# A cached-attention decode kernel: softmax and value product of the last row block taken group by group

## The chip, the cores and the metric

The kernel runs on 1 core of one Trainium2 chip. The metric is device time in microseconds (us). Before the change it was 705.47 us (median of 4 runs, 705.14 to 706.13).

## The reference, cut to what matters

One decode step of a transformer layer: layer norm, grouped attention against a cache, residual, layer norm, MLP, residual.

```python
q = (layernorm(x) @ wq)                       # 16 query heads of 256, one token
k, v = k_cache, v_cache                       # 8 groups x 32768 rows x 256, bf16, each used by 2 query heads
p = softmax(q @ k.T * 256 ** -0.5)            # over 32768 rows
h = x + (p @ v) @ wo                          # 4096 -> 448
h1 = layernorm(h) @ w1 + b1                   # 448 -> 1792
out = h + (h1 * tanh(softplus(h1))) @ w2      # 1792 -> 448
```

The two caches are 268 MB together and every byte is used once. With the weights the kernel reads 279 MB.

## The kernel before

The 32768 rows are taken in 16 row blocks of 2048 (`NR = 16`). For each row block `r` and group `g`, a 1 MB K tile is loaded, transposed on VectorE (DVE) and multiplied on TensorE (PE); the scores of all 8 groups of a row block gather in one PSUM tile `s`. Then one `chain(r)` makes the softmax of the whole row block: maximum on DVE, combined across partitions on GpSimd (POOL), exponential on ScalarE (ACT). The V products of row block `r - 1` run interleaved with the K work of row block `r`. Each is an `o` tile of 64x512, merged into the running sum `ACC` on DVE.

```python
NKN, NKT, NVN, NO = 4, 3, 4, 3                # ring sizes: K tiles, transposed K, V tiles, o tiles
s_ring = [...]                                # 2 score tiles
for r in range(NR + 1):
    if r == NR: flush_pending()
    for g in range(G):
        if r < NR:  k_unit(g, r)              # load K, transpose, 8 matmuls into s_ring[r % 2]
        if r >= 1:  v_unit(g, r - 1)          # load V, 8 matmuls of 512 columns into o
        ...
    if r < NR: chain(r)                       # softmax of the row block, all groups together
```

In the last pass (`r == NR`) only V products are left. There, each group's product is merged with `ACC`, scaled by the inverse denominator, transposed and projected, in series:

```python
    # v_unit, last row block
    for t2 in range(T // 2):
        nc.tensor.matmul(o[:], lhsT=pt[...64 columns...], rhs=vn[...512 columns...], ...)
    dv(nc.vector.scalar_tensor_tensor(out=ob[:], in0=ACC[:, g, :], scalar=fin["a2"][0:64, 0:1], in1=o[:], ...))
    for dh in range(2):
        nc.tensor.matmul(oT_ps[:, dh, :], lhsT=ob[...], rhs=ident_bf[...2 columns...], ...)   # twice
    nc.scalar.copy(out=og[:], in_=oT_ps[:])
    project(og, [2 * g, 2 * g + 1])           # 4 matmuls of 1x448 into h_ps, with wo
```

After that come the layer norm of `h_ps`, the MLP and the store (called the epilogue below). `ld` issues loads from the SP queue in program order, and `dv` keeps DVE's order as written.

## Time and profile before

| what | before | view |
|---|---|---|
| span of the profiled run | 703.4 us | page, first line |
| DMA stream full, about 427 GB/s | from 66 to about 664 us, ends at 667 | slices, windows |
| last K tile begins its transpose | 645.4 us | timeline |
| first of the last eight V products | 656.4 us | timeline |
| last project matmul ends | 685.4 us | timeline |
| epilogue | 18.0 us | timeline |

The slice rows of the page of before divide the span into 40 slices of 17.6 us; a digit is the busy share in tenths, and PEclk is the granted clock of TensorE.

```profile
PE   2842787777877777787777877787777777777785
...
PEclk9975999999999999999999999999999999999996
DMA  8999999999999999999999999999999999999800
GB/s 328 417 361 330 424 429 424 427 429 425 427 428 426 428 427 425 427 425 428 427 426 428 427 427 427 427 426 427 426 428 425 428 428 425 428 426 426 369 0 1
```

The DMA row is 9 nearly to the end, while PE has slack: the stream is the limit until the second slice from the end. Of the time after its end, 703.4 - 667 = 36 us, none is hidden. The timeline of before shows how the tail is spent (columns: start, duration in us, engine, source line, operation, output and inputs; in brackets the idle time before it and what ended that).

```profile
645.41 2.31 DVE L216 STREAM_TRANSPOSE kt<-kn 128x2048 f32<-128x2048 f32 x1 [2.04 <-DMA kn<-in_A_k_cache_dram]
...
647.77 1.90 PE L224 MATMUL s<-kt,QTall 128*128 128x512 bf16 x8 [1.23 <-DVE kt L216]
...
653.09 0.69 ACT L245 ACTIVATE p<-s,NMrun 128x512 bf16<-128x512 f32 x1 [38.28 <-POOL NMrun L243]
...
656.42 4.68 PE L291 MATMUL o<-kn,pt 128*64 128x512 bf16 x13 [1.46 <-DVE pt L267]
...
684.48 0.92 PE L275 MATMUL h_ps<-wo_sb,og 128*1 128x448 bf16 x4 [0.31 <-ACT og L312]
685.44 0.52 ACT L341 COPY h_sb<-h_ps 1x448 f32<-1x448 f32 x1 [1.01 <-PE h_ps L275]
```

The last K tile is transposed at 645.41. The softmax of the whole row block then takes until 656.4, and only then do the eight last V products start, though about half of their data is there (an estimate from the rates in the windows: 427 GB/s to 664 and 249 to 667 leave about 4.0 of 8.4 MB to land). The line with `o<-kn` is a V product too: the first four of the last V tiles are loaded into K buffers in before. The products end at 684.48 + 0.92 = 685.4.

The windows of before give, for a stretch of time, its length, the busy time of PE, of PE's weight loads, of DVE, ACT and POOL, each with its number of instructions, and then the granted clock, the DMA share and GB/s.

```profile
652.00:656.00 4.00, 0.35 (x2) 0.30 (x2) 1.41 (x7) 1.16 (x4) 0.82 (x4) 1.00 1.01 428
656.00:660.00 4.00, 3.58 (x9) 1.51 (x10) 0.52 (x2) 0.00 (x0) 0.00 (x0) 0.59 1.02 430
660.00:664.00 4.00, 4.00 (x21) 1.50 (x19) 1.33 (x2) 0.16 (x1) 0.00 (x0) 0.99 1.01 426
...
694.00:698.00 4.00, 2.81 (x8) 0.97 (x9) 0.93 (x5) 0.06 (x1) 0.00 (x0) 0.50 0.00 0
```

PE was idle for most of 652 to 656. The clock then fell to half at about 656.7 and came back at about 660.1 (windows). In the epilogue it stayed at half although PE was busy 2.81 of 4 us.

### The profile page before, as it was taken

Reading aid. Unit: us, or ns where it says so; the run is one execution under the profiler, and the core shown is the slowest. Engines: PE = TensorE matmul, PEld = TensorE weight load, DVE = VectorE, ACT = ScalarE, POOL = GpSimd, SP = SyncE. Lnnn points to the kernel's source line nnn. Section 1 sums busy time; section 2 is a strip of 40 time slices with the busy share of each in tenths; the row PEclk is TensorE's granted clock in tenths of the full one; section 3 lists DMA queues with packets and bytes.
Section 4 is the critical chain, followed back from the end, with each engine's and each line's share of the span. In section 5 each row is a group of like instructions: output and inputs, shape, how many; then the busy total and the mean of one; then the engine's idle time right before and its main releaser. Section 6 shows DMA issues by size and latency. Waiting matters only on the chain.

```text
span 703.4 us, 5939 instructions
## 1 busy us (share of the span) xinstructions
PE 513.2 (73%) x2322; PEld 214.1 (30%) x2322; DVE 406.7 (58%) x324; ACT 22.0 (3%) x68; POOL 35.5 (5%) x157
## 2 busy tenths in 40 slices
PE   2842787777877777787777877787777777777785
PEld 2310333333333333233333333333333333333223
DVE  2922565656666575666657575666657565665222
ACT  2000000000000000000000000000000000000000
POOL 1010010000101010100101010100101010100100
PEclk9975999999999999999999999999999999999996
DMA  8999999999999999999999999999999999999800
GB/s 328 417 361 330 424 429 424 427 429 425 427 428 426 428 427 425 427 425 428 427 426 428 427 427 427 427 426 427 426 428 425 428 428 425 428 426 426 369 0 1
DMA packets 45648, 279.39 MB, mean 397 GB/s; under 512 B 6066, under 2 KB 11956, under 8 KB 12404
## 3 DMA queue, kind: packets, MB, share of 16 engines
q1 hardware_dynamic: 45620, 279.01, 95.3%
q8 instruction: 18, 0.29, 0.1%
q14 instruction: 10, 0.08, 0.0%
HBM read 278.99 MB, written 0.00 MB: 397 GB/s over the span
## 4 chain that ended last, share of the span: by engine, by line
DMA 76%; DVE 12%; PE 5%; SPq 5%; issue 1%; POOL 0%; ACT 0%; DVEq 0%; POOLq 0%; ACTq 0%
DMA kn<-in_A_k_cache_dram 76%; DVE kt L216 11%; SPq L72 5%; PE o L291 2%; PE h_ps L275 1%; PE o_ps L370 1%; DVE ob L303 1%; PE h1T_ps L350 1%; PE s L224 0%; PE oT_ps L307 0%; ACT p L245 0%; DVE hn_bf L143 0%; DVEq L216 0%; DVE pt L267 0%; DVE g L232 0%
## 5 line engine op out<-in xcount | busy, mean ns | idle before, releaser
L216 DVE STREAM_TRANSPOSE kt<-kn 128x2048 f32<-128x2048 f32 x128 | 295.6, 2310 | 208.8 <-DMA kn<-in_A_k_cache_dram 208.3
L224 PE MATMUL s<-kt,QTall 128*128 128x512 bf16 x1024 | 248.1, 384 | 164.4 <-DVE kt L216 164.4
L291 PE MATMUL o<-vn,pt 128*64 128x512 bf16 x992 | 239.9, 384 | 0.2
L224 PEld LDWEIGHTS <-QTall 128*128 128x128 bf16 x1024 | 98.2, 97 | 311.2 <-issue 192.9
L291 PEld LDWEIGHTS <-pt 128*64 128x64 bf16 x1024 | 102.6, 110 | 139.6 <-issue 52.7
L299 DVE SCALAR_TENSOR_TENSOR ACC<-ACC,alpha_all,o 64x512 f32<-64x512 f32 x112 | 78.2, 698 | 1.7 <-PE o L291 1.7
L234 POOL COPY g<-g 32x1 f32<-32x1 f32 x48 | 8.4, 176 | 609.9 <-DVE g L232 608.3
L245 ACT ACTIVATE p<-s,NMrun 128x512 bf16<-128x512 f32 x16 | 11.0, 688 | 622.4 <-POOL NMrun L243 622.4
L232 DVE TENSOR_REDUCE g<-s 128x1 f32<-128x512 f32 x16 | 11.1, 692 | 23.4 <-PE s L224 23.4
L303 DVE SCALAR_TENSOR_TENSOR ob<-ACC,a,o 64x512 bf16<-64x512 f32 x8 | 5.9, 739 | 21.6 <-PE o L291 21.6
L270 DVE STREAM_TRANSPOSE pt<-p 128x512 bf16<-128x512 bf16 x15 | 10.7, 711 | 9.5 <-ACT p L245 9.5
L291 PE MATMUL o<-kn,pt 128*64 128x512 bf16 x32 | 9.9, 448 | 1.5 <-DVE pt L267 1.5
L243 POOL COPY NMrun<-NMrun 32x1 f32<-32x1 f32 x48 | 8.6, 178 | 2.3
L177 PE MATMUL qT_ps<-xnT,vn 128*128 128x1 bf16 (+1 forms) x128 | 4.0, 165 | 5.4 <-DMA vn<-in_A_wq_dram 5.4
L275 PE MATMUL h_ps<-wo_sb,og 128*1 128x448 bf16 x32 | 7.3, 351 | 0.3 <-ACT og L312 0.3
L370 PE MATMUL o_ps<-w_sb,actT 128*1 128x448 bf16 x14 | 5.4, 574 | 1.9 <-DVE actT L367 1.9
L188 DVE COPY Qin<-qrow_ps 32x128 bf16<-32x128 bf16 x2 | 0.6, 280 | 10.2 <-PE qrow_ps L182 9.8
L236 POOL TENSOR_SCALAR t<-g 32x1 f32<-32x1 f32 x16 | 5.8, 361 | 1.7
L297 DVE COPY ACC<-o 64x512 f32<-64x512 f32 x8 | 5.2, 649 | 0.6 <-PE o L291 0.6
L177 PEld LDWEIGHTS <-vn 128*128 128x128 bf16 (+1 forms) x128 | 3.7, 104 | 5.7 <-DMA vn<-in_A_wq_dram 5.7
L238 POOL TENSOR_SCALAR NM_all<-t,g 32x1 f32<-32x1 f32 x16 | 4.6, 289 | 1.5
L240 POOL TENSOR_SCALAR NMrun<-NMrun,NM_all 32x1 f32<-32x1 f32 x16 | 4.5, 284 | 1.5
(74 smaller groups left out, 48.4 us busy)
## 6 DMA issues: line engine op xcount, KB each, us to landing
kn<-in_A_k_cache_dram SPq DMA_DIRECT2D x128, 1024.0 KB, 17.2
vn<-in_A_v_cache_dram SPq DMA_DIRECT2D x124, 1024.0 KB, 15.8
kn<-in_A_v_cache_dram SPq DMA_DIRECT2D x4, 1024.0 KB, 12.9
wo_sb<-in_A_wo_dram SPq DMA_DIRECT2D x1, 3584.0 KB, 19.8
vn<-in_A_wq_dram SPq DMA_DIRECT2D x3, 1024.0 KB, 6.8
w_sb<-in_B_w_dram SPq DMA_DIRECT2D x1, 1568.0 KB
w_sb<-in_B_w_dram SPq DMA_DIRECT2D x3, 448.0 KB, 8.5
vn<-in_A_wq_dram SPq DMA_DIRECT2D x1, 512.0 KB
```

Source lines behind the costliest of these rows:

```text
L72: inst = nc.sync.dma_start(out=out_ap, in_=in_ap)
L216: dv(nc.vector.transpose(out=kt_[:].rearrange("p t d -> p (t d)").bitcast(F32), in_=kn[:].rearrange("p t d -> p (t d)").bitcast(F32)))
L224: nc.tensor.matmul(s[:], lhsT=QTall[:, g, x_of(j, e), :], rhs=ktv[:, :, j, :, e], start=(g == 0 and i == 0), stop=(g == G - 1 and i == 7))
L232: dv(nc.vector.reduce_max(out=g4[:, 0:1], in_=s[:], axis=AX.X))
L243: nc.gpsimd.tensor_copy(out=NMrun[32 * q:32 * q + 32, r + 1:r + 2], in_=NMrun[0:32, r + 1:r + 2])
L245: nc.scalar.activation(out=p_[:], in_=s[:], func=ACT.Exp, bias=NMrun[:, r + 1:r + 2], scale=1.0, accum_out=L_all[:, r:r + 1])
L270: pending.append(lambda: dv(nc.vector.transpose(out=pt[:].rearrange("p t c -> p (t c)"), in_=p_[:])))
L275: nc.tensor.matmul(h_ps[:], lhsT=o_bf[:, dh, ci:ci + 1], rhs=wo_sb[:, c * 2 + dh, :], start=False, stop=False, skip_group_check=True)
L291: nc.tensor.matmul(o[:], lhsT=pt[:, 2 * t2:2 * t2 + 2, :].rearrange("p t c -> p (t c)"), rhs=vn[:, 2 * t2:2 * t2 + 2, :].rearrange("p t d ...
L299: dv(nc.vector.scalar_tensor_tensor(out=ACC[:, g, :], in0=ACC[:, g, :], scalar=alpha_all[0:64, r:r + 1], in1=o[:], op0=ALU.mult, op1=ALU.add))
L303: dv(nc.vector.scalar_tensor_tensor(out=ob[:], in0=ACC[:, g, :], scalar=fin["a2"][0:64, 0:1], in1=o[:], op0=ALU.mult, op1=ALU.add))
L370: nc.tensor.matmul(o_ps[:], lhsT=actT[:, ft:ft + 1], rhs=w2_sb[:, ft, :], start=(ft == 0), stop=(ft == FT - 1))
```

## The change

The intent is to shorten the tail. The softmax of the last row block is taken per group, right after that group's K tile, so that the last V products no longer wait for all groups. Each last V load comes three groups later (`LAG = 3`) between the other loads. The last product is computed directly in transposed form: the V tile is the stationary operand and only two columns of p move. This removes `o`, the merge on DVE and the separate transposes; `ACC`, scaled on ACT (`obp`), is added by four narrow matmuls. "Narrow" is used below for matmuls that move only one or two columns, and also for project, which moves 448 columns but has one column stationary; "dense" or "wide" ones move 512 columns and have 64 or 128 stationary. The diff, cut to its core:

```diff
-    NKN, NKT, NVN, NO = 4, 3, 4, 3
+    NKN, NKT, NVN, NO = 4, 3, 4, 2
...
+    def chain_last(g, between=None):          # softmax of one group of the last row block
+        s = s_ring[g % 2]
+        nm = cross_quadrant_negmax(s, between)
...      (masked maximum, exp with a per-group bias, alpha, W)
+        def chain_b():
...          (denominator: DVE, one matmul, DVE reciprocal)
+            nc.scalar.activation(out=p_[:], in_=p_[:], func=ACT.Identity, scale=rden[:, 0:1])
+            nc.scalar.activation(out=obp[:], in_=ACC[:, g, :], func=ACT.Identity, scale=a2[0:64, 0:1])
+        def b3():
+            dv(nc.vector.transpose(out=pt[...], in_=p_[:]))
+        return chain_b, b3
...
+    def v_unit_last(g):
+        vn = vn_ring[n % NVN]
+        ld(vn[:], A_v_cache[0, g, (NR - 1) * RB:NR * RB, :]...)
...      (4 narrow matmuls that add obp)
+        for dh in range(2):
+            for t in range(T):
+                nc.tensor.matmul(oT_ps[:, g, dh, :], lhsT=vn[:, t, dh * P:(dh + 1) * P],
+                                 rhs=pt[:, t, 2 * g:2 * g + 2], ...)
+        nc.scalar.copy(out=og[:], in_=oT_ps[:, g])
+        return lambda: project(og, [2 * g, 2 * g + 1])
...
-    for r in range(NR + 1):
...
+    for r in range(NR - 1):
...      (as before)
+    with tc.manual_schedule(engines={PE, Activation}):
+        for g in range(G):
+            k_unit(g, NR - 1, s_ring[g % 2], first=True, lastmm=True)
+            if proj: proj()
+            cur = chain_last(g, prev[0] if prev else None)
+            v_unit(g, NR - 2)
+            proj = v_unit_last(g - LAG) if g >= LAG else None
+            if prev: pending.append(prev[1])
+            prev = cur
+        flush_pending()
+        proj()
+        v_unit_last(G - LAG)()
+        prev[0]()
+        prev[1]()
+        for g in range(G - LAG + 1, G):
+            v_unit_last(g)()
```

`manual_schedule` fixes the order of PE and ACT as written. A few start-up operations on DVE and more order tokens are left out here.

More of the change, by code (lines that the diff above doesn't have):

```diff
@@ L111 @@
     NM_all = const.tile([P, NR], F32)
-    L_all = const.tile([P, NR], F32)
-    NMrun = const.tile([P, NR + 1], F32)
+    L_all = const.tile([P, NR + G - 1], F32)
+    NMrun = const.tile([P, NR + G], F32)
     nc.vector.memset(NMrun[:, 0:1], BIG)
@@ L120 @@
     o_ring = [ps_ring.tile([64, 512], F32, name=f"o{i}") for i in range(NO)]
+    oT_ps = ps_ring.tile([P, G, 2, 2], F32)
+    nc.vector.memset(oT_ps[:], 0.0)
+    pt_last = [const.tile([P, T, 32], BF16, name=f"ptl{i}") for i in range(G)]
+    obp_all = [const.tile([64, 512], BF16, name=f"obp{i}") for i in range(G)]
+    maskrow = const.tile([P, 16], F32)
+    nc.vector.tensor_reduce(out=maskrow[:], in_=ident_f[:].rearrange("p (q g hh) -> p g q hh", q=4, g=16, hh=2),
+                            axis=AX.XY, op=ALU.add)
+    negbigrow = const.tile([P, 16], F32)
+    nc.vector.tensor_scalar(out=negbigrow[:], in0=maskrow[:], scalar1=-1.0, scalar2=BIG, op0=ALU.add, op1=ALU.mult)
+    bigposrow = const.tile([P, 16], F32)
+    nc.vector.tensor_scalar(out=bigposrow[:], in0=maskrow[:], scalar1=-BIG, scalar2=BIG, op0=ALU.mult, op1=ALU.add)
     p_ring = [const.tile([P, T * 32], BF16, name=f"p{i}") for i in range(2)]
@@ L167 @@
     row_to_cols(xn_bf, xnT, D, token=True)
+    NPRE = 0
+    for n in range(NPRE):
+        ld(kn_ring[n % NKN][:], A_k_cache[0, n, 0:RB, :].rearrange("(p t) d -> p t d", p=P))
+        dv(nc.vector.transpose(out=kt_ring[n % NKT][:].rearrange("p t d -> p (t d)").bitcast(F32),
+                               in_=kn_ring[n % NKN][:].rearrange("p t d -> p (t d)").bitcast(F32)))
     qT_ps = ps_m.tile([P, NCH], F32, tag="m")
@@ L187 @@
         if i % 2 == 0:
-            nc.vector.tensor_copy(out=o_ap, in_=i_ap)
+            dv(nc.vector.tensor_copy(out=o_ap, in_=i_ap))
         else:
@@ L191 @@
     QX = const.tile([P, P], BF16)
-    nc.vector.transpose(out=QX[:], in_=Qin[:])
+    dv(nc.vector.transpose(out=QX[:], in_=Qin[:]))
     for i in range(4):
@@ L195 @@
         src = _ap(QX, 32 * i, 32, 0, [[2, G], [16, 8], [1, 2]])
-        nc.vector.tensor_copy(out=dst, in_=src)
+        dv(nc.vector.tensor_copy(out=dst, in_=src))
     def x_of(j, e):
@@ L208, in flush_pending, with k_unit @@
             pending.pop(0)()
-    def k_unit(g, r):
+    def k_unit(g, r, s, first, lastmm):
         n = state["nk"]
@@ L213, in k_unit @@
         kn = kn_ring[n % NKN]
-        ld(kn[:], A_k_cache[0, g, r * RB:(r + 1) * RB, :].rearrange("(p t) d -> p t d", p=P))
         kt_ = kt_ring[n % NKT]
-        dv(nc.vector.transpose(out=kt_[:].rearrange("p t d -> p (t d)").bitcast(F32),
-                               in_=kn[:].rearrange("p t d -> p (t d)").bitcast(F32)))
+        if n >= NPRE:
+            ld(kn[:], A_k_cache[0, g, r * RB:(r + 1) * RB, :].rearrange("(p t) d -> p t d", p=P))
+            dv(nc.vector.transpose(out=kt_[:].rearrange("p t d -> p (t d)").bitcast(F32),
+                                   in_=kn[:].rearrange("p t d -> p (t d)").bitcast(F32)))
         flush_pending()
-        s = s_ring[r % 2]
         ktv = kt_[:].rearrange("p t (j b e) -> p t j b e", j=4, b=32, e=2)
@@ L224, in k_unit, with cross_quadrant_negmax @@
                 nc.tensor.matmul(s[:], lhsT=QTall[:, g, x_of(j, e), :], rhs=ktv[:, :, j, :, e],
-                                 start=(g == 0 and i == 0), stop=(g == G - 1 and i == 7))
+                                 start=(first and i == 0), stop=(lastmm and i == 7))
                 i += 1
-    def chain(r):
-        last = (r == NR - 1)
-        s = s_ring[r % 2]
+    def cross_quadrant_negmax(s, between=None):
         g4 = small.tile([P, 4], F32, tag="g4")
         dv(nc.vector.reduce_max(out=g4[:, 0:1], in_=s[:], axis=AX.X))
+        if between is not None:
+            between()
         for q in range(1, 4):
@@ L237, in chain @@
                                 op0=ALU.max, op1=ALU.max)
-        nc.gpsimd.tensor_scalar(out=NM_all[0:32, r:r + 1], in0=t1[:, 0:1], scalar1=g4[0:32, 3:4], scalar2=-1.0,
+        nm = small.tile([32, 1], F32, tag="nm")
+        nc.gpsimd.tensor_scalar(out=nm[:], in0=t1[:, 0:1], scalar1=g4[0:32, 3:4], scalar2=-1.0,
                                 op0=ALU.max, op1=ALU.mult)
-        nc.gpsimd.tensor_scalar(out=NMrun[0:32, r + 1:r + 2], in0=NMrun[0:32, r:r + 1], scalar1=NM_all[0:32, r:r + 1],
+        return nm
+    def chain(r):
+        s = s_ring[r % 2]
+        nm = cross_quadrant_negmax(s)
+        nc.gpsimd.tensor_scalar(out=NMrun[0:32, r + 1:r + 2], in0=NMrun[0:32, r:r + 1], scalar1=nm[:, 0:1],
                                 scalar2=None, op0=ALU.min)
@@ L249, in chain @@
         pt = pt_ring[r % 2]
-        if last:
-            W = small.tile([P, NR], F32, tag="W")
-            nc.scalar.activation(out=W[:], in_=NMrun[:, 1:NR + 1], func=ACT.Exp, bias=NMrun[:, NR:NR + 1], scale=-1.0)
-            junk = small.tile([P, NR], F32, tag="junk")
-            denp = small.tile([P, 1], F32, tag="denp")
-            rden = const.tile([P, 1], F32, name="rden")
-            a2 = const.tile([P, 1], F32, name="a2")
-            fin["a2"] = a2
-            def fin_ops():
-                dv(nc.vector.scalar_tensor_tensor(out=junk[:], in0=W[:], scalar=1.0, in1=L_all[:], op0=ALU.mult,
-                                                  op1=ALU.mult, accum_out=denp[:]))
-                den_ps = ps_m.tile([P, 1], F32, tag="m")
-                nc.tensor.matmul(den_ps[:], lhsT=sel2[:], rhs=denp[:], start=True, stop=True)
-                dv(nc.vector.reciprocal(out=rden[:], in_=den_ps[:]))
-                dv(nc.vector.tensor_tensor(out=a2[:], in0=alpha_all[:, r:r + 1], in1=rden[:], op=ALU.mult))
-                dv(nc.vector.tensor_scalar(out=p_[:], in0=p_[:], scalar1=rden[:, 0:1], scalar2=None, op0=ALU.mult))
-                dv(nc.vector.transpose(out=pt[:].rearrange("p t c -> p (t c)"), in_=p_[:]))
-            pending.append(fin_ops)
-        else:
-            pending.append(lambda: dv(nc.vector.transpose(out=pt[:].rearrange("p t c -> p (t c)"), in_=p_[:])))
@@ new lines, in chain @@
+        pending.append(lambda: dv(nc.vector.transpose(out=pt[:].rearrange("p t c -> p (t c)"), in_=p_[:])))
+    def chain_last(g, between=None):
+        jL = NR - 1 + g
+        jN = NR + g
+        s = s_ring[g % 2]
+        nm = cross_quadrant_negmax(s, between)
+        nmm = small.tile([32, 1], F32, tag="nmm")
+        nc.gpsimd.tensor_scalar(out=nmm[:], in0=nm[:], scalar1=maskrow[0:32, g:g + 1], scalar2=bigposrow[0:32, g:g + 1],
+                                op0=ALU.mult, op1=ALU.add)
+        nc.gpsimd.tensor_scalar(out=NMrun[0:32, jN:jN + 1], in0=NMrun[0:32, jN - 1:jN], scalar1=nmm[:, 0:1],
+                                scalar2=None, op0=ALU.min)
+        for q in range(1, 4):
+            nc.gpsimd.tensor_copy(out=NMrun[32 * q:32 * q + 32, jN:jN + 1], in_=NMrun[0:32, jN:jN + 1])
+        biasg = small.tile([P, 1], F32, tag="biasg")
+        nc.scalar.activation(out=biasg[:], in_=NMrun[:, jN:jN + 1], func=ACT.Identity,
+                             scale=maskrow[:, g:g + 1], bias=negbigrow[:, g:g + 1])
+        p_ = p_ring[g % 2]
+        nc.scalar.activation(out=p_[:], in_=s[:], func=ACT.Exp, bias=biasg[:, 0:1], scale=1.0,
+                             accum_out=L_all[:, jL:jL + 1])
+        alphag = small.tile([P, 1], F32, tag="alphag")
+        nc.scalar.activation(out=alphag[:], in_=NMrun[:, jN - 1:jN], func=ACT.Exp, bias=NMrun[:, jN:jN + 1], scale=-1.0)
+        W = small.tile([P, NR + G - 1], F32, tag="W")
+        nc.scalar.activation(out=W[:, 0:jL + 1], in_=NMrun[:, 1:jL + 2], func=ACT.Exp, bias=NMrun[:, jN:jN + 1],
+                             scale=-1.0)
+        pt = pt_last[g]
+        def chain_b():
+            junk = small.tile([P, NR + G - 1], F32, tag="junk")
+            denp = small.tile([P, 1], F32, tag="denp")
+            dv(nc.vector.scalar_tensor_tensor(out=junk[:, 0:jL + 1], in0=W[:, 0:jL + 1], scalar=1.0,
+                                              in1=L_all[:, 0:jL + 1], op0=ALU.mult, op1=ALU.mult, accum_out=denp[:]))
+            den_ps = ps_m.tile([P, 1], F32, tag="m")
+            nc.tensor.matmul(den_ps[:], lhsT=sel2[:], rhs=denp[:], start=True, stop=True)
+            rden = small.tile([P, 1], F32, tag="rden")
+            dv(nc.vector.reciprocal(out=rden[:], in_=den_ps[:]))
+            a2 = small.tile([P, 1], F32, tag="a2")
+            dv(nc.vector.tensor_tensor(out=a2[:], in0=alphag[:], in1=rden[:], op=ALU.mult))
+            nc.scalar.activation(out=p_[:], in_=p_[:], func=ACT.Identity, scale=rden[:, 0:1])
+            obp = obp_all[g]
+            nc.scalar.activation(out=obp[:], in_=ACC[:, g, :], func=ACT.Identity, scale=a2[0:64, 0:1])
+        def b3():
+            dv(nc.vector.transpose(out=pt[:].rearrange("p t c -> p (t c)"), in_=p_[:]))
+        return chain_b, b3
@@ L280, in v_unit @@
         state["nv"] += 1
-        last = (r == NR - 1)
-        if last:
-            vn = kn_ring[g % NKN] if g < NKN else vn_ring[n % NVN]
-        else:
-            vn = vn_ring[n % NVN]
+        vn = vn_ring[n % NVN]
         ld(vn[:], A_v_cache[0, g, r * RB:(r + 1) * RB, :].rearrange("(p t) d -> p t d", p=P))
@@ L297, in acc @@
                 dv(nc.vector.tensor_copy(out=ACC[:, g, :], in_=o[:]))
-            elif not last:
+            else:
                 dv(nc.vector.scalar_tensor_tensor(out=ACC[:, g, :], in0=ACC[:, g, :], scalar=alpha_all[0:64, r:r + 1],
                                                   in1=o[:], op0=ALU.mult, op1=ALU.add))
-            else:
-                ob = small.tile([64, 512], BF16, tag="ob")
-                dv(nc.vector.scalar_tensor_tensor(out=ob[:], in0=ACC[:, g, :], scalar=fin["a2"][0:64, 0:1], in1=o[:],
-                                                  op0=ALU.mult, op1=ALU.add))
-                oT_ps = ps_m.tile([P, 2, 2], F32, tag="m")
-                for dh in range(2):
-                    nc.tensor.matmul(oT_ps[:, dh, :], lhsT=ob[:, dh * P:(dh + 1) * P],
-                                     rhs=ident_bf[0:64, 2 * g:2 * g + 2], start=True, stop=False)
-                    nc.tensor.matmul(oT_ps[:, dh, :], lhsT=ob[:, 256 + dh * P:256 + (dh + 1) * P],
-                                     rhs=ident_bf[0:64, 32 + 2 * g:32 + 2 * g + 2], start=False, stop=True)
-                og = small.tile([P, 2, 2], BF16, tag="og")
-                nc.scalar.copy(out=og[:], in_=oT_ps[:])
-                project(og, [2 * g, 2 * g + 1])
@@ L314, in v_unit @@
-        if last:
-            acc()
-        else:
-            pending.append(acc)
+        pending.append(acc)
+    def v_unit_last(g):
+        n = state["nv"]
+        state["nv"] += 1
+        vn = vn_ring[n % NVN]
+        ld(vn[:], A_v_cache[0, g, (NR - 1) * RB:NR * RB, :].rearrange("(p t) d -> p t d", p=P))
+        pt = pt_last[g]
+        obp = obp_all[g]
+        for dh in range(2):
+            nc.tensor.matmul(oT_ps[:, g, dh, :], lhsT=obp[:, dh * P:(dh + 1) * P],
+                             rhs=ident_bf[0:64, 2 * g:2 * g + 2], start=False, stop=False, skip_group_check=True)
+            nc.tensor.matmul(oT_ps[:, g, dh, :], lhsT=obp[:, 256 + dh * P:256 + (dh + 1) * P],
+                             rhs=ident_bf[0:64, 32 + 2 * g:32 + 2 * g + 2], start=False, stop=False,
+                             skip_group_check=True)
+        for dh in range(2):
+            for t in range(T):
+                nc.tensor.matmul(oT_ps[:, g, dh, :], lhsT=vn[:, t, dh * P:(dh + 1) * P], rhs=pt[:, t, 2 * g:2 * g + 2],
+                                 start=False, stop=False, skip_group_check=True)
+        og = small.tile([P, 2, 2], BF16, tag="og")
+        nc.scalar.copy(out=og[:], in_=oT_ps[:, g])
+        return lambda: project(og, [2 * g, 2 * g + 1])
@@ L325, in load_epilogue_weights @@
         ld(b1T[:], B_b1.rearrange("(k p) -> p k", p=P))
-    for r in range(NR + 1):
-        if r == NR:
-            flush_pending()
+    for r in range(NR - 1):
         for g in range(G):
-            if r < NR:
-                k_unit(g, r)
+            k_unit(g, r, s_ring[r % 2], first=(g == 0), lastmm=(g == G - 1))
             if r >= 1:
@@ L336 @@
                 load_epilogue_weights()
-        if r < NR:
-            chain(r)
+        chain(r)
+    prev = None
+    proj = None
+    LAG = 3
+    with tc.manual_schedule(engines={mybir.EngineType.PE, mybir.EngineType.Activation}):
+        for g in range(G):
+            k_unit(g, NR - 1, s_ring[g % 2], first=True, lastmm=True)
+            if proj:
+                proj()
+            cur = chain_last(g, prev[0] if prev else None)
+            v_unit(g, NR - 2)
+            proj = v_unit_last(g - LAG) if g >= LAG else None
+            if prev:
+                pending.append(prev[1])
+            prev = cur
+        flush_pending()
+        proj()
+        v_unit_last(G - LAG)()
[3 more added lines that the diff above has]
+            v_unit_last(g)()
     h_sb = const.tile([1, D], F32)
```

## The prediction

> **What bounds the kernel now.** The slice table shows DMA engines full at about 427 GB/s from 66 us to about 666 us, while PE and DVE have slack (the group table gives DVE 208 us of waiting for K tiles). Nothing the change does reduces the 279 MB, so the streaming part stays. What can move is the tail. The timeline of the tail of before: the last K tile lands at 645.4; softmax of the last row block (K transpose 2.31, matmuls 1.9, maximum, POOL chain, exp, denominator, p transpose) takes until 656.4; only then do the eight last V products start, although their data has been landing since 648; they are serial at 3.46 us each (o 1.9, ob 0.74, oT, og, h_ps 0.92) until the last h_ps at 685.4; then layer norm, the MLP and the store take 18.0 us. So 19 us of PE and DVE work run after the DMA stream is empty, plus 18 us that the change does not touch.
>
> **What the change does.** In the last row block each group gets its own softmax right after its K tile, its last V load is interleaved three groups later, and the last V product goes straight into the transposed form: 32 matmuls 2 columns wide, for which I take 32 ns each (the 128x1 wq matmuls, 32 in 1.01 us), about 1.2 us a group, in place of o + ob + oT. Added per group: maximum 0.69, denominator ops about 1.0 on DVE, a POOL chain of about 3.0, ACT about 3. DVE then needs 2.31+1.9+0.7+1.1+gaps = 6.1 us per group and PE's order about 6.5. With three 1 MB loads per group (2.43 us each, 7.3) the DMA remains the limit for groups 3 to 7; groups 0 to 2 (4.9 us of DMA) fall behind by a few us, which the buffers absorb. The o ring of 2, the extra start-up DVE ops and the token ordering should cost nothing visible: the ACC update already ends before the next o product begins.
>
> **Cost of the interleave.** The last K tile now lands about four loads later, at about 655. From there, worked out from the durations above: maximum done 660, V of row block 14 done 662.6, which frees the buffer for the last load (lands 667). After the loop PE's fixed order runs in series: project(4), product 5 and project(5), denominator of group 7, scale p (0.7) and ACC (0.6) on ACT, product and project 6, product and project 7. I estimate the last h_ps at 674.4 instead of 685.4, so 11 us gained. But this end has only narrow matmuls. The Trainium skill, "TensorE: Matmul & The Clock Gate", Part 1, says that the array falls to half clock after an idle window of about 3.4 us; this trace agrees (0.50 after the gap at 652, and it stayed 0.50 from 688 to 701 in spite of busy narrow matmuls). If the clock falls before products 6 and 7, that costs up to 4 us. I take 1 us.
>
> **Predicted:** 695.5 us, range 692 to 700 (about -1.4%). Faster by over 2%: 0.10; within 2%: 0.88; slower: 0.02.
>
> **What would show it.** Right: DMA full until about 667, groups in the last block spaced at about 7 us, last h_ps near 674-676, an epilogue of still 18 us at half clock. A higher gain: chain of waits ends in the last V load and h_ps ends by 670.
>
> **What would make it wrong.** The four V buffers now serve two loads per group; if PE's round is over 7.3 us, loads are issued late and DMA holes appear after 625. The narrow matmuls could cost 73 ns (as in the h1T product at half clock). ACT could be late with scaling p, holding PE. A table reload for Identity would make it much worse.

## The result, and the profile after

The changed kernel took 698.21 us (median of 9 runs, 695.89 to 699.50), against 705.67 us for before in the same rounds. The ratio is 0.989, with a 95% interval of 0.9878 to 0.9902. Ratios here are those from the runs of both kernels in the same rounds; they are not quite the ratio of the medians. This is a clear 1.1%. The time lies in the predicted range, but the gain is 7.5 us of the 10 predicted (705.67 - 698.21, against 705.5 - 695.5). The profiled run was the slowest of the nine (699.5 us, span 697.7).

The same slice rows of the page of after:

```profile
PE   3751877777777777777777778787877778778885
...
PEclk9995999999999999999999999999999999999965
DMA  8999999999999999999999999999999999999930
```

The stream now ends at about 671 us rather than 667, later in the shorter span. PEclk shows something new: the clock is down in the last two slices (0.6 and 0.5), where before had that in the last only. The timeline of after, at the start of the last row block, and then at its end:

```profile
616.12 3.36 PE L241 MATMUL s<-kt,QTall 128*128 128x512 bf16 x8 [2.41 <-ACT p L268]
```

```profile
657.98 2.31 DVE L234 STREAM_TRANSPOSE kt<-kn 128x2048 f32<-128x2048 f32 x1 [1.87 <-DMA kn<-in_A_k_cache_dram]
...
660.34 3.44 PE L241 MATMUL s<-kt,QTall 128*128 128x512 bf16 x8 [1.72 <-DVE kt L234]
...
665.04 1.91 PE L334 MATMUL o<-vn,pt 128*64 128x512 bf16 x8
...
669.37 0.92 PE L322 MATMUL h_ps<-wo_sb,og 128*1 128x448 bf16 x4 [1.34 <-ACT og L364]
...
671.66 1.65 PE L322 MATMUL h_ps<-wo_sb,og 128*1 128x448 bf16 x4 [0.25 <-ACT og L364]
...
673.25 0.59 PE L306 MATMUL den_ps<-denp,sel 128*128 128x1 f32 x2
...
675.57 1.65 PE L322 MATMUL h_ps<-wo_sb,og 128*1 128x448 bf16 x4 [0.59 <-ACT og L364]
...
677.34 1.01 PE L361 MATMUL oT_ps<-ptl,vn 128*128 128x2 bf16 x32
...
678.60 1.65 PE L322 MATMUL h_ps<-wo_sb,og 128*1 128x448 bf16 x4 [0.25 <-ACT og L364]
...
680.29 0.52 ACT L406 COPY h_sb<-h_ps 1x448 f32<-1x448 f32 x1 [1.74 <-PE h_ps L322]
```

Four things can be read here. First, at 616.12 PE had waited 2.41 us for the exp (`p`) of row block 14. Second, the last K tile is transposed at 657.98, and PE multiplies it in 3.44 us instead of 1.9: half clock. Third, the denominator of group 7 (673.25) stands in PE's order behind two projects. Fourth, the last projects take 1.65 us instead of 0.92. The last ends at 680.3, 5.1 us sooner than in before; the epilogue is 17.4 us (18.0 in before).

The windows of after over its tail:

```profile
666.00:670.00 4.00, 2.65 (x45) 1.54 (x43) 1.55 (x4) 2.35 (x8) 1.30 (x6) 1.00 0.53 166
670.00:674.00 4.00, 3.75 (x49) 2.16 (x48) 0.13 (x1) 0.16 (x1) 0.00 (x0) 0.54 0.27 115
674.00:678.00 4.00, 3.41 (x66) 2.06 (x65) 0.91 (x3) 1.38 (x3) 0.00 (x0) 0.50 0.01 4
```

PE is busy 3.75 and 3.41 of 4 us and yet the clock is down at 0.50. Busy PE and granted clock are two different readings. The Trainium skill, "Trainium Kernel Development and Optimization", section "Performance Expectations", warns that matmul busy time is a bad metric of distance to the roofline because matmuls are pipelined; here there is a second reason, with these numbers.

### The profile page after: what moved, and what is told of

Read it like the earlier page. It is cut to its first block, busy times and chain, and to the rows that moved or that the text cites. A ratio compares the mean times of both kernels' runs of the same rounds, so it can differ in the third digit from the quotient of the medians. Undisturbed runs are those within 1.5% of the kernel's fastest.

```text
span 697.7 us, 6510 instructions
## 1 busy us (share of the span) xinstructions
PE 510.6 (73%) x2528; PEld 217.5 (31%) x2528; DVE 412.2 (59%) x361; ACT 43.2 (6%) x120; POOL 52.4 (8%) x228
## 4 chain that ended last, share of the span: by engine, by line
DMA 72%; DVE 14%; PE 6%; SPq 5%; issue 1%; ACT 1%; POOL 1%; DVEq 0%; POOLq 0%; ACTq 0%
DMA kn<-in_A_k_cache_dram 70%; DVE kt L234 12%; SPq L72 5%; PE s L241 2%; DMA vn<-in_A_wq_dram 2%; PE h_ps L322 1%; PE o_ps L435 1%; DVE g L247 1%; PE h1T_ps L415 1%; PE oT_ps L361 1%; PE o L334 1%; PE den_ps L306 0%; POOL g L251 0%; PE qT_ps L194 0%; DVE QTall L213 0%
## 5 line engine op out<-in xcount | busy, mean ns | idle before, releaser
L241 PE MATMUL s<-kt,QTall 128*128 128x512 bf16 x1024 | 252.1, 389 | 161.9 <-DVE kt L234 159.5
L334 PE MATMUL o<-vn,pt 128*64 128x512 bf16 x960 | 230.9, 383 | 0.2
L334 PEld LDWEIGHTS <-pt 128*64 128x64 bf16 x960 | 96.1, 110 | 127.3 <-issue 45.0
L251 POOL COPY g<-g 32x1 f32<-32x1 f32 x69 | 12.2, 176 | 603.6 <-DVE g L247 601.3
L247 DVE TENSOR_REDUCE g<-s 128x1 f32<-128x512 f32 x23 | 15.9, 692 | 32.9 <-PE s L241 32.9
L361 PE MATMUL oT_ps<-ptl,vn 128*128 128x2 bf16 x256 | 7.8, 164 | 0.0
L361 PEld LDWEIGHTS <-vn 128*128 128x128 bf16 x256 | 7.1, 99 | 0.1
L311 ACT ACTIVATE p<-p,rden 128x512 bf16<-128x512 bf16 x8 | 5.8, 722 | 19.9 <-DVE rden L308 19.9
L256 POOL TENSOR_SCALAR nm<-t,g 32x1 f32<-32x1 f32 x23 | 6.7, 290 | 2.2
L316 DVE STREAM_TRANSPOSE ptl<-p 128x512 bf16<-128x512 bf16 x8 | 5.6, 695 | 0.7 <-ACT p L311 0.7
```

Of the source, the lines that this page charges most:

```text
L241: nc.tensor.matmul(s[:], lhsT=QTall[:, g, x_of(j, e), :], rhs=ktv[:, :, j, :, e], start=(first and i == 0), stop=(lastmm and i == 7))
L247: dv(nc.vector.reduce_max(out=g4[:, 0:1], in_=s[:], axis=AX.X))
L251: nc.gpsimd.tensor_copy(out=g4[0:32, q:q + 1], in_=g4[32 * q:32 * q + 32, 0:1])
L334: nc.tensor.matmul(o[:], lhsT=pt[:, 2 * t2:2 * t2 + 2, :].rearrange("p t c -> p (t c)"), rhs=vn[:, 2 * t2:2 * t2 + 2, :].rearrange("p t d ...
L361: nc.tensor.matmul(oT_ps[:, g, dh, :], lhsT=vn[:, t, dh * P:(dh + 1) * P], rhs=pt[:, t, 2 * g:2 * g + 2], start=False, stop=False, skip_gr ...
```

## The experiments

All kernels gave correct results. Each ratio is to the kernel before in the same rounds.

| run | what | median us | ratio | 95% interval |
|---|---|---|---|---|
| after | the change | 698.21 | 0.9890 | 0.9878 to 0.9902 |
| e1 | after, score and p buffers swapped | 696.71 | 0.9876 | 0.9862 to 0.9889 |
| e2 | after, five V buffers | 696.86 | 0.9878 | 0.9861 to 0.9896 |
| e3 | before, only the narrow last product | 700.97 | 0.9936 | 0.9923 to 0.9948 |
| e4 | after, dummy matmuls in the tail | 694.66 | 0.9862 | 0.9839 to 0.9886 |
| e5 | after, other PE order in the tail | 695.15 | 0.9850 | 0.9835 to 0.9866 |
| e6 | e1 + e2 + e5 | 695.44 | 0.9862 | 0.9839 to 0.9885 |
| e7 | e3, dummy matmuls | 698.47 | 0.9898 | 0.9865 to 0.9931 |
| e8 | e6, dummy matmuls | 694.04 | 0.9838 | 0.9823 to 0.9853 |
| e9 | after, wide last product | 701.89 | 0.9946 | 0.9933 to 0.9959 |
| e10 | before, two o buffers | 705.63 | 0.9999 | 0.9984 to 1.0014 |
| e11 | e8, b1 loaded in rows | 694.58 | 0.9831 | 0.9812 to 0.9850 |
| e12 | e11, more dummies | 690.67 | 0.9802 | 0.9787 to 0.9818 |

### Which half of the change brings the gain: e3 and e9

e3 leaves the loads and the softmax of before and only makes the last product narrow.

```diff
 # before, v_unit, last row block; NO = 2 to free a PSUM bank for oT_ps
-        (8 matmuls into o, merge on DVE, 4 narrow matmuls, og, project)
+        obp = ACC[:, g, :] * a2                      # on ACT
+        (4 narrow matmuls of obp, 32 narrow matmuls of V, og, project)
```

> Before, with only the last V product put in the narrow transposed form (32 matmuls of 2 columns, ACC scaled on ACT), softmax of the last block still once for all groups, loads in the order of before. Theory N: most of the gain of the change comes from the shorter product per group (3.46 us to about 2.4), the interleave pays back what it gains by landing the last K tile 10 us later; then the last h_ps ends at 675 to 678 and the kernel takes 695 to 698, as little as after. Rival I: the gain comes from the per-group softmax; then the narrow product alone gains under 3 us (over 702.5).

It gained 0.64%, about 4.5 us, which falls between the two theories as they were stated. e9 is the opposite: the per-group softmax and the interleave of after, with the wide product.

```diff
 # after, v_unit_last
-        (4 narrow matmuls of obp, 32 narrow matmuls of V)
+        (8 matmuls of 512 columns into o; the merge into ob on DVE is queued behind the next K transpose;
+         oT, og and project come one group later)
```

> After with the narrow last product undone: the per-group softmax, the interleaved loads and the lag of 3 stay, but each last V product is again the wide one (8 matmuls of 512 columns, then the ACC merge of 0.74 us on DVE, then oT, og and project, taken up one group later). Theory: in the interleaved form the narrow product is worth its shorter PE time in the three products behind the loop, about 0.8 us each plus the DVE merge of 0.74 on the path, but it also lets the clock fall; net 1 to 4 us slower than after, 699 to 702, with the clock at 1.0 longer. Rival: the narrow form is the main gain (as much as e3's 4.4 us or more); then 703 or slower.

It gained 0.54%, about 3.8 us; 701.89 lies in the range that its theory gave. So each half alone brings about half: 0.64% and 0.54%, together 1.18%, and the change as a whole brings 1.10%. Neither is "the main gain", and within their intervals they add. In its profile e9 has the clock at 1.00 in all windows from 640 to 680 and is still slower than after: its stream carries 389 GB/s from 640 to 656 (after: 411) and its last project ends at 683.2. Full clock alone is not what makes the tail short. In the profile of e9 PE's round from one K product to the next is 7.07 us (639.77 to 646.85), against 5.99 in after (640.50 to 646.49):

```profile
639.77 1.91 PE L240 MATMUL s<-kt,QTall 128*128 128x512 bf16 x8
...
646.85 1.91 PE L240 MATMUL s<-kt,QTall 128*128 128x512 bf16 x8
```

### The half clock of the tail: e3, e4 and e7

e3's profile explains why it did not gain more. Its windows:

```profile
656.00:664.00 8.00, 6.82 (x116) 4.04 (x116) 0.72 (x2) 5.20 (x11) 0.00 (x0) 0.50 1.01 425
664.00:672.00 8.00, 7.31 (x88) 3.38 (x88) 0.00 (x0) 0.40 (x3) 0.00 (x0) 0.50 0.25 102
672.00:680.00 8.00, 7.08 (x118) 4.05 (x116) 0.00 (x0) 0.49 (x3) 0.00 (x0) 0.50 0.01 2
```

After the idle time of the softmax the clock falls to half as in before, but here it never comes back: for 24 us PE is busy about 7 of 8 us with narrow matmuls and stays at 0.50. In before it came back with the wide products. About half of each group's 3.04 us is project (1.65 us); which of the two kinds of narrow matmul keeps the clock down is not separated. e7 adds dense dummy matmuls (128x512, results never read) to e3.

```diff
+            burn(s_ring[1], 4)        # in the softmax gap, before the denominator
             flush_pending()
+            burn(s_ring[1], 6)        # after it
...
+            burn(s_ring[1], 2)        # in each group, while og is copied
             project(og, [2 * g, 2 * g + 1])
```

> e3 (before with only the narrow last product) with dummy dense matmuls: 10 in PE's idle time of the last softmax and 2 in each group's wait for its copy. Theory: e3 gained only 4.4 us because with narrow products the array stayed at half clock for the whole tail (project 1.65 us, 3.05 us a group); warm, a group takes about 2.5 us and the kernel about 696 to 697.5. Rival: the half clock is not what costs there; then 701 or slower.

The median of 698.47 is above the expected range, with runs from 695.65 to 700.94. The profiled run (700.94, the slowest) shows why. The clock came back at about 658.2, held at 1.00 and is 0.50 again from about 671.9 on, in the middle of groups of the same kind. While it is up, a group takes 2.37 us (project from 662.89 to 665.25 and 667.62), against 3.04 in e3 (658.05 to 661.09); when it falls, 3.6. So the mechanism was right, and two dense matmuls a group did not hold it to the end in this run. The times alone do not show the gain over e3, for the two intervals overlap a little. The instructions of `h_ps` in both, with the shortest, the median and the longest duration in ns (the duration of one overlaps the next, so four take 0.92 or 1.65 us):

```profile
L278 PE MATMUL h_ps<-wo_sb,og x32: 530/577/581, 658.1 to 680.6; 128*1 128x448 bf16 x32
```

```profile
L283 PE MATMUL h_ps<-wo_sb,og x32: 350/352/578, 660.5 to 681.0; 128*1 128x448 bf16 x32
```

e4 puts dummies into the tail of after itself.

```diff
         flush_pending()
+        burn(s_ring[0], 5)
         proj()
-        v_unit_last(G - LAG)()
+        p5 = v_unit_last(G - LAG); burn(s_ring[0], 1); p5()
...      (2 before each later project, 12 in the layer norm gap, 7 in the MLP gap)
```

> After, with dummy dense 128x512 matmuls (results never read) in PE's idle slots of the tail: 5 before project of group 4, 1 or 2 before the other projects, 12 in the layer norm gap, 7 in the MLP gap. Theory: the tail pays for half clock because its matmuls are narrow; with the dummies the clock stays 1.0, project takes 0.92 instead of 1.65 us, the final 14 matmuls 3.0 to 3.4 instead of 4.9 to 5.4 us, and the kernel takes 3 to 4 us less than after (694 to 695). Rival: the clock in the tail does not follow dense work or the dummies cost what they bring; then 698 or slower.

The median is as expected, 694.66, though one run of five was at 698.57 and the interval is wide. With work added to PE and none removed, the medians differ by about 3.5 us; by the ratios it is 0.28%, about 2 us, and the intervals touch (0.9878 and 0.9886), so the times make the gain likely and do not show it alone. Its windows from 664 to 680:

```profile
664.00:672.00 8.00, 7.53 (x129) 4.30 (x128) 2.57 (x7) 3.31 (x11) 0.83 (x5) 1.00 0.52 197
672.00:680.00 8.00, 7.84 (x62) 3.16 (x63) 1.54 (x5) 0.68 (x2) 0.77 (x2) 0.79 0.00 0
```

The clock is 1.00 (after: 0.90) and then 0.79 (after: 0.50). Three of the last four projects take 0.92 us, where after has 1.65 for three of four, and the last 14 matmuls take 2.96 us (after: 4.86). Half clock is therefore a real cost in the tail of the profiled runs, and the dummies restore most of it there.

### The start of the last row block and the V buffers: e1 and e2

```diff
-            k_unit(g, NR - 1, s_ring[g % 2], ...)                  # chain_last: s_ring[g % 2], p_ring[g % 2]
+            k_unit(g, NR - 1, s_ring[(g + NR - 1) % 2], ...)       # chain_last: the same index
```

> After, with the score and p buffers of the last row block chosen as (g+15) mod 2, so that group 0 of the last block does not take the score buffer that the softmax of row block 14 is still reading. Theory: that reuse made PE wait 2.4 us for the exp at 613.7 and then run the eight K matmuls at half clock (3.36 instead of 1.9 us), and the lag of about 2.6 us made later V loads be issued late. Then the wait and the half-clock run vanish, the last K tile lands 1 to 2 us earlier and the kernel takes 1 to 2 us less than after (about 696.5). Rival: the buffers absorb the lag; wait gone, time unchanged within 0.5 us (about 698).

Row block 14 has its scores in `s_ring[0]`, and after gave `s_ring[0]` to group 0 of row block 15 as well. e1 removes the 2.41 us wait for the exp, as its line for the same K product shows:

```profile
614.40 1.91 PE L241 MATMUL s<-kt,QTall 128*128 128x512 bf16 x8 [1.23 <-DVE kt L234]
```

Here PE waits 1.23 us for the transpose, as it does throughout the stream. The half clock of this product is another matter: e2, e4 and e5 keep the shared buffer and the wait (2.39 to 2.42 us), and there it took 3.44, 2.73 and, in e5, 1.90 us:

```profile
614.60 1.90 PE L241 MATMUL s<-kt,QTall 128*128 128x512 bf16 x8 [2.39 <-ACT p L268]
```

So the wait of 2.4 us comes from the buffer, but whether the clock falls in it differs from run to run. The last K tile of e1 is transposed at 656.6 (after: 658.0). That is no measure of the repair by itself: e4 and e5, the same program as after up to its tail, have 656.9 and 655.6. The time went from 698.21 to 696.71, near what was expected, but the two intervals overlap, so this gain is likely and not shown.

```diff
-    NKN, NKT, NVN, NO = 4, 3, 4, 2
+    NKN, NKT, NVN, NO = 4, 3, 5, 2      # pt_last and obp then rotate through 4 buffers each, to make room
```

> After, with five V buffers instead of four (the per-group p and ACC tiles of the last block rotate through four buffers to make room). Theory: the DMA dips between 632 and 650 (307 to 414 GB/s in some 2 us slices, together about 1.5 us of stream) come from V loads that wait for a V buffer. With five they vanish, the last K tile lands about 656.5 instead of 658.0, the last load about 668 instead of 671, and the kernel takes 1.5 to 3 us less than after (695 to 696.5). Rival: the end of the kernel is bound by PE's fixed order after the loop and not by landing times; then the time changes by less than 0.7 us.

In e2 the last K tile is transposed at 655.0. The windows from 612 to 660, of after, of e1 and of e2:

```profile
612.00:660.00 48.00, 38.02 (x288) 18.01 (x287) 33.77 (x53) 20.01 (x54) 18.46 (x79) 0.96 0.99 415
```

```profile
612.00:660.00 48.00, 37.37 (x291) 17.89 (x290) 34.78 (x55) 20.00 (x54) 18.31 (x79) 1.00 1.01 424
```

```profile
612.00:660.00 48.00, 39.13 (x293) 18.30 (x292) 34.32 (x56) 20.00 (x54) 17.68 (x76) 0.96 1.01 424
```

The stream carries 424 GB/s in e1 and in e2, and 415, 416 and 418 in after, e4 and e5, which have neither repair. So either repair alone takes most of the dips away: they came from four V buffers together with the lag of group 0, not from the number of buffers alone. Counted from the first K tile of the last row block, the last one is transposed after 44.6 us in e1 and 44.0 in e2, against 45.4, 45.7 and 44.5 in after, e4 and e5: up to about 1 us. The time of e2, 696.86, lies just above the expected range, and again its interval overlaps that of after.

### PE's order behind the loop: e5 and e6

```diff
         flush_pending()
-        proj()                       # project 4
-        v_unit_last(G - LAG)()       # product 5, project 5
-        prev[0](); prev[1]()         # denominator of group 7, transpose of its p
-        for g in range(G - LAG + 1, G):
-            v_unit_last(g)()         # product 6, project 6, product 7, project 7
+        p4 = proj
+        p5 = v_unit_last(5)
+        prev[0](); prev[1]()
+        p4(); p6 = v_unit_last(6); p5(); p7 = v_unit_last(7); p6(); p7()
```

> After, with only PE's fixed order behind the loop changed: product 5, denominator of group 7, project 4, product 6, project 5, product 7, project 6, project 7 (before: project 4, product 5, project 5, denominator 7, product 6, project 6, product 7, project 7). Theory: in after the denominator of group 7 sat at 673.2 behind a project although its inputs were ready at 669.5, and each project waited for its own copy; then the end of the last project moves 3 us (at half clock) to 4 us earlier and the kernel takes 694 to 695.5. Rival: the end is set by the landing of the last V tile or of the last K tile; then under 1 us gained (over 697).

e5 is the only single repair whose gain is shown by the times: 695.15, 0.9850, its interval wholly below that of after. Its profile has the denominator of group 7 at 666.44, 5.25 us after the o product of group 7 of row block 14 (661.19); in after the same distance is 673.25 - 665.04 = 8.2 us.

```profile
661.19 1.91 PE L334 MATMUL o<-vn,pt 128*64 128x512 bf16 x8
...
666.44 0.36 PE L306 MATMUL den_ps<-denp,sel 128*128 128x1 f32 x2
...
671.40 3.15 PE L322 MATMUL h_ps<-wo_sb,og 128*1 128x448 bf16 x8
...
674.58 0.52 ACT L410 COPY h_sb<-h_ps 1x448 f32<-1x448 f32 x1 [2.92 <-PE h_ps L322]
```

The last eight project matmuls still take 3.15 us, which is half clock.

> After with the three repairs together: score and p buffers swapped, five V buffers, the tail order of e5. If the three act at different places (start of the last block, loads, tail), the gains add: about 1.4 + 1.3 + 3.5 = 6 us, so 691.5 to 693. If they all hide behind one limit, such as the stream end at 667 to 668, the sum is smaller: about 694.

The three repairs together (no other edit) are no better than e5 alone: 695.44, outside both ranges that were expected. In e6's profile the stream has no dips, and the last K tile is transposed at 655.99; but PE then ran part of the last K product at half clock, and the last project ends at 675.6. In that run the clock took back what the better stream gives; that this holds for the other runs is not shown.

### Both together: e8, e11 and e12

e8 is e6 with dummies: 3 before the denominator of group 7, 3 before product 7, 1 before project 7, and 12 and 7 in the epilogue's gaps.

> e6 with dummy dense matmuls in idle slots of the tail and of the layer norm and MLP gaps. Theory: half clock costs e6 about 1 to 2 us in projects and 2 us in the last 14 matmuls; then 3 us below e6, about 689 to 690, over 2% faster than before. Rival: 0 to 1 us below e6.

694.04 is 1.4 us below e6, between theory and rival, and the two intervals overlap. The clock is 1.00 from 656 to 680, and the 14 last matmuls take 3.40 us (after: 4.86). But it fell to 0.89 between 640 and 656, inside the row block, where e8 has no dummies.

e11 adds something from outside the change. In before the profile has a dip of the stream between 44 and 66 us, where the 3.5 KB bias `b1` is loaded as 1792 pieces of 2 bytes.

```diff
-        ld(b1T[:], B_b1.rearrange("(k p) -> p k", p=P))
+        ld(b1r[:], B_b1.rearrange("(k p) -> k p", p=P))     # 14 rows of 128; transposed by PE in the epilogue
```

> e8 with one thing from outside the change: the bias b1 is loaded as 14 contiguous rows of 128 and transposed by PE in the layer norm gap, instead of as 1792 pieces of 2 bytes. Theory: the profile of before shows a dip to 300 to 350 GB/s between 44 and 66 us in which that load was issued and after which K loads came 20 us late; the dip shrinks and the kernel gains 3 to 6 us on e8, 688 to 691, clear of 2%. Rival: the dip comes from the other weight loads (rows of 896 bytes and less) that share the window; then under 1.5 us gained.

The stream did gain. The same window in before and in e11:

```profile
53.00:66.00 13.00, 0.00 (x0) 0.00 (x0) 2.23 (x1) 0.00 (x0) 0.00 (x0) 0.50 0.98 300
```

```profile
53.00:66.00 13.00, 0.88 (x3) 0.32 (x3) 2.88 (x2) 0.00 (x0) 0.00 (x0) 0.50 1.05 373
```

The rate rose from 300 to 373 GB/s, and the last K tile is transposed 2.3 us earlier than in e8 (654.5 against 656.8). The time did not follow: 694.58, no gain on e8. The Trainium skill, "DMA: Bandwidth & Descriptors", section "Specifications", asks for at least 512 B a transfer for line rate; the trace agrees, in that packets under 512 B between 26 and 70 us fell from 2033 to 269 as the rate rose. The profile of e11, taken in the slowest of its five runs (696.20), shows where the gain went in that run:

```profile
646.87 2.31 DVE L235 STREAM_TRANSPOSE kt<-kn 128x2048 f32<-128x2048 f32 x1 [1.80 <-DMA kn<-in_A_k_cache_dram]
...
649.24 3.55 PE L242 MATMUL s<-kt,QTall 128*128 128x512 bf16 x8 [1.66 <-DVE kt L235]
```

DVE waited 1.80 us for the K tile of group 6, PE stood idle 1.66 us, and then ran the product at half clock. The runs fit this: the two quickest (692.14 and 693.12) have a mean clock of 0.978, the three others 0.968 to 0.970. e12 puts four dummies at the end of the rounds of groups 3 to 6 and four before product 5.

```diff
             proj = v_unit_last(g - LAG) if g >= LAG else None
+            if LAG <= g < G - 1:
+                burn(s_ring[(g + NR) % 2], 4)
...
+        burn(s_ring[1], 4)
         p5 = v_unit_last(5)
```

> e11 with 4 more dummy dense matmuls at the end of each round of groups 3 to 6 and 4 before product 5 (the dummies now read a weight tile that is never rewritten). e11 gained nothing on e8 although its stream was about 2 us ahead: PE waited 1.7 us for the K tile of group 6 with only narrow matmuls behind it, fell to half clock, ran those K matmuls in 3.55 us, and was at half clock again in the tail. Theory: the clock takes back what the earlier stream gives; with the dummies the clock is 1.0 through the last block and the tail, K matmuls stay at 1.9 us and project at 0.92, and the kernel takes 689.5 to 691.5, 2% or more below before. Rival: PE's round gets too long (over 7.3 us) or the clock falls all the same; then 693 or slower.

690.67 us, 0.9802: the best kernel of the study, 15 us below before and twice the gain of the change. Its interval spans the 2% limit, so by that limit its verdict is unclear. Its windows:

```profile
640.00:648.00 8.00, 7.82 (x77) 3.98 (x77) 5.15 (x9) 3.54 (x9) 3.19 (x15) 1.00 1.01 424
648.00:656.00 8.00, 7.75 (x93) 4.28 (x93) 5.37 (x9) 3.65 (x10) 2.67 (x12) 1.00 1.02 429
656.00:664.00 8.00, 7.42 (x68) 3.59 (x66) 4.33 (x12) 3.81 (x13) 2.31 (x10) 1.00 0.93 389
664.00:672.00 8.00, 7.84 (x131) 4.79 (x131) 1.05 (x5) 1.82 (x5) 0.00 (x0) 1.00 0.08 33
```

The clock is 1.00 from 640 to 672, and the last project ends at 672.4. Its runs are also closer together, 690.34 to 692.60 (e11: 692.14 to 696.20).

### The control: e10

```diff
-    NKN, NKT, NVN, NO = 4, 3, 4, 3
+    NKN, NKT, NVN, NO = 4, 3, 4, 2
```

> Before with two o buffers instead of three and nothing else. Theory: free, the ACC update ends before the next o product starts in the stream; within 0.5 us of before. Rival: the smaller ring costs part of what the change gains; over 1 us slower.

The ratio is 0.9999, with an interval of 0.9984 to 1.0014: the smaller o ring costs nothing that these runs can show.

## Why the prediction was right, and where its sizes were off

| step | predicted | measured in the profile of after |
|---|---|---|
| stream limits until the last row block, unchanged | yes | yes, 427 GB/s from 100 to 612 us; dips from 632 us on |
| spacing of the groups in the last row block | about 7 us, set by the DMA | 6.0 to 6.4 us for groups 1 to 6, 7.9 for group 7 |
| narrow product | about 1.2 us, 32 ns a matmul | 32 in 0.95 us, 30 ns, with obp about 1.1 us |
| PE's round, groups 4 to 6 | about 6.5 us | 5.99 us |
| last K tile | about 655 | transposed at 657.98 |
| V product of row block 14, group 7, done | 662.6 | 667.0 |
| last load landed | 667 | about 671 |
| last project done | 674.4, with 1 us more for the clock | 680.3 |
| epilogue | 18.0 us | 17.4 us |

- The mechanism was right in the main: the stream stays as it is, the tail becomes shorter, and interleaving delays the last K tile. Right also were the small gain (under 2%), the free o ring (e10), and the fear of half clock at the end. That the time fell into the range owes something to its width of 8 us: the last project ended 5.9 us later than the 674.4 of the sum, which had 1 us in hand for the clock. Of these, 3.0 us are the late last K tile, 1.4 us come between it and the last V product of row block 14 (its K product at half clock), and 1.5 us in PE's series after that. ACT's Identity did not reload its table (one load in the whole trace, as in before); the Trainium skill, "ScalarE: Activation LUTs", section "Table sets: the hidden batching unit", says that cheap functions such as identity are in every set, and this trace agrees.
- "If the clock falls before products 6 and 7, that costs up to 4 us. I take 1 us." This term of the sum was too small. In the profiled run the last K product took 3.44 us instead of 1.9 and three projects 1.65 instead of 0.92, which is 1.5 + 3 x 0.73 = 3.7 us before the epilogue. e4 won 2 us (by the ratios) to 3.5 us (by the medians) back with dummies alone, in the tail and the epilogue. Also too narrow was the place where I looked: the clock already fell at the last K tile, and in other runs within the row block. Nor does it take an idle window of 3.4 us, as the prediction has it from the skill: in after the clock fell at about 660.1, in an idle gap of 1.72 us, and at about 670.3, 1 us behind a gap of 1.34 us, each time with narrow matmuls before the gap. The measurement decides here.
- "Groups 0 to 2 fall behind by a few us, which the buffers absorb" was half wrong. PE waited 2.41 us for a score buffer that row block 14 still held, which I had not looked for, and together with this lag four V buffers for two V loads a group let the stream dip from 632 us on. PE, once behind, and not the DMA then set the pace: its K products of groups 4 to 6 follow each other at 5.99 us without a wait. In e1, without the lag, the last three come at 7.0 to 7.4 us, near the 7.3 that the prediction had from the loads. The last K tile of e1 was 1.4 us and that of e2 3.0 us earlier than in after, but much of that is chance: in the profiled run of after, the slowest, the last row block started 1.45 us later than in before (K tile of group 0 transposed at 612.59, not 611.14), while e2, e4, e5 and e9, with the same start-up, have 610.98 to 611.26.
- The order of PE after the loop was in the prediction as a series of waits, but taken as given. It is worth about 3 us (e5).
- The narrow matmuls were expected to slow to 73 ns at half clock in the worst case. They did not: 32 took 1.01 us at half clock, against 0.95.
- Not settled: how much of the spread of after (695.89 to 699.50; before 704.71 to 706.33) is due to the clock. The five slowest of its nine runs have a mean granted clock of 0.958 to 0.961 over the whole span, the four fastest 0.963 to 0.971. That fits, but those runs are known only by their means. The Trainium skill, "TensorE: Matmul & The Clock Gate", Part 1, says that the activity window of about 3.4 us is free-running, so it would fall differently in each run; no run here tests that, though it fits that the K product after the 2.4 us wait took 3.36, 2.73 and 1.90 us in after, e4 and e5, which are one program up to there. Nor is it separated which of the parts of e12 its gain needs. Its step from e11 is 3.9 us between the medians, but the two intervals still overlap a little (0.9787 to 0.9818, and 0.9812 to 0.9850); that of e8 (0.9823 to 0.9853) does not overlap.

## What to carry to other kernels

When a stream bounds a kernel, its tail is what can be won, and the tail must be costed with the clock that it will really have: replacing wide matmuls by narrow ones saves columns but can leave the array at half clock for everything after. A few dense dummy matmuls in slots where PE waits anyway are a cheap test for this, and in e12, with the repairs, they kept the clock up. When a loop is split, check by index which buffer the first new iteration shares with the last old one, and write the order of an in-order engine by when its inputs are ready, not group by group.

## What the Trainium skill lacked or had wrong

- "TensorE: Matmul & The Clock Gate", Part 1, says that the clock rises after about 3.4 us of sustained busy time. Outside transpose mode it does not say that a PE kept busy with narrow matmuls may not count as busy for this: in e3 PE was busy 6.82, 7.31 and 7.08 of 8 us in three windows, and the clock stayed 0.50 in all of them. With wide products (128x512) it came back 3.4 us after it fell (656.7 to 660.1 in before, 660.1 to 663.5 in after), as the page says.
- The same page names idle gaps of about 3 us and more as what lets the clock fall, and has nothing on how much dense work holds it. In after it fell within a gap of 1.72 us. In e7 two 128x512 matmuls per 2.37 us held it from about 660 to about 672 and then no longer; in e12, with four dummies written (three of them in the records) in a round of about 6.9 us, besides the 16 dense matmuls of the K and V products, it was 1.00 from 640 to 672.
- The same page, Part 1, "Wait — 56ns, not 53.3ns?", gives a smallest pitch of 25 ns or about 62 ns a matmul, depending on how instructions are decoded. With a new stationary operand for each, 32 matmuls of 2 columns took 0.95 us at full and 1.01 us at half clock, about 30 ns each; yet 56 matmuls of 1 column in the MLP took 4.08 us at half clock and 3.81 us at full (e8), about 70 ns each. No page that I read explains the difference between the two.
